# Two attentions on one core: value groups 4 to 7 of the dense units in one 512-column visit, the next x between the last Q and K

## The chip, the cores and the metric

One core of a Trainium2 chip. The metric is the device time of one execution in microseconds (us), median of several runs; lower is better. The engines are named as the profile names them: PE is TensorE (PEld its weight loads), DVE VectorE, ACT ScalarE, POOL GpSimd, SP SyncE.

## The reference

Two independent attentions over 2048 positions, model width 1024, 32 heads of 32. Each projects x to Q, K and V, attends and multiplies with wo; the two outputs stand side by side.

```
qkv = x @ wqkv                                   # (2048, 3072), q, k, v of 32 heads of 32
A: logits at keys pos - 0, 2, .., 14             # 8 keys, every second position
   softmax, weighted sum of v, @ wo
B: scores = q @ k.T / sqrt(32), masked to 0 <= i - j < 256
   softmax, @ v, @ wo
return concatenate([a, b], axis=-1)              # (1, 2048, 2048), float32
```

## The kernel before

The work is cut into eight units of 512 positions. Units 0 to 3 are B, the dense units; units 4 to 7 are A, the window units, whose positions are sorted into even and odd ones, so that the window of every second key becomes one of neighbours. A unit has eight groups of four heads (NG = 8); a group takes part as one "head" s below, and hg = 8 u + s numbers them through.

Every matmul of projections is made of three (TERMS): both operands are split into a high part, rounded to fp32r, and a rest, and high x high, high x rest and rest x high are added up. The split is made on the chip: a load of 512 KB lands in a tile of the ring `raws` (three tiles, tag raw), a cast on ACT (L213) or DVE (L216) makes the high part and two subtractions on DVE (L219) the rest, into the pools `wpool` (three tiles) or `xpool` (nine tiles of 512 columns, eight of which are one unit's x).

The projections form one list of visits, in the order of `plan`: per head a Q and a K visit (`qk_items`, L577, 8 steps of 3 matmuls of 512 columns each), value visits in between (`v_items`, L645), and for dense units the output projection of the unit before (`o_items`, L705). A value visit covers several groups at once. VPARTS says which: groups 0 to 3 in one wide visit (four weights of two k-steps by 512 columns; each of two rounds goes through the weights, and the first quarter is loaded and split twice, so five loads; matmuls of 512 columns), groups 4 and 5, and 6 and 7, in a narrow one each (two loads, matmuls of 256 columns). V_SLOTS says after which head's Q and K a visit stands: 0, 5 and 7 (V0_SLOTS for unit 0: 1, 3 and 7). The last narrow visit carries the arrival of the next unit's x: the four x loads are split after steps 1, 5, 9 and 13 (XAT = 1, m = 4), because the old x tiles come free one after the other.

Attention of a dense head runs in two halves: 16 score matmuls (L1078) for row maxima and sums (L1083 on DVE, L1088 on ACT), one small matmul for the row sums (L1117), which DVE spreads (L1123) into extra rows of Q, then transposed scores (L1161), exponentials (L1168), masks on POOL (L1147) or DVE (L1150), and the product with the values (L1208). A window head copies its rows from a tile of the ring `natp` (three tiles, tag nat) to its seat by SP's queue (pbuf<-nat), has many small score matmuls (L914), a chain on DVE and ACT (L922 to L964) in a buffer `band`, and the product with the values (L975).

The output projection of the window units is done at the end, for pairs of units (4 and 5, 6 and 7), as seven products (`product`, L764, 48 matmuls of 512 columns each) of sums of attention outputs with sums of weights. The sums are made in the background: `weight_sums` and `output_sums` load two pieces each by SP's queue (L832, r<-od, r<-wo), add on DVE (L837) and store again (L843) to sd and td, from where products load them like any other weight or x. Unit pair 4 and 5 had its `output_sums` after heads 4 to 7 of unit 5, pair 6 and 7 after heads 4 to 7 of unit 7.

The order of instructions on every engine is fixed when the program is made: a planner (class `Clock`) keeps an estimated time for each engine and each transfer, and always takes the one of four lists (row sums, second halves, first halves, projections) whose next item can start first. Loads go out on POOL's queue (`Stream.load_to`), each after the split that frees its tile; `split_to` makes the splits when a visit nears. A dictionary of gates holds loads back until their source is written. PE has three accumulator banks for projections (tag g), four for scores (s) and one for values (o).

## Time and profile before

| | |
|---|---|
| median of 3 runs | 1830.73 us (1830.16 to 1833.35) |
| the profiled execution's own time | 1835.97 us |
| its span | 1834.0 us |
| granted TensorE clock, mean | 0.991 |
| PE busy | 1799.3 us (98%) |
| DVE, ACT, POOL busy | 1262.2, 925.6, 409.2 us |
| DMA | 303.61 MB, mean 166 GB/s |

Busy time of an engine is the time in which at least one of its instructions runs. A row of a timeline gives the start, the duration, engine, line, operation, tiles and count, and in brackets the idle time before it with what ended it; runs of one operation are merged. A row of windows gives the busy time and instruction count of PE, PEld, DVE, ACT and POOL in a stretch, then the granted clock (PEclk, 1.00 is full), the DMA share and GB/s. A row of lines gives the busy time, the mean of one instruction in ns and the idle time ahead of it. "issue" means that the engine waited for nothing that the profile shows.

### The profile page before, as it was taken

The page shows a single profiled execution, that of the slowest core. Times are in us where ns is not written, and L with a number is a line of the kernel's source. Part 1 is how long each engine was busy: PE and PEld are TensorE (multiplying, and loading weights), DVE is VectorE, ACT ScalarE, POOL GpSimd, SP SyncE. Part 2 cuts the span into 40 slices and gives each one's busy share as a digit, 9 for nine tenths or more (in the row PEclk, how much of TensorE's full clock was granted, in tenths as well). Part 3 has the DMA queues.
Part 4 walks back from the last instruction along what each step waited for, and adds up shares of the span by engine and source line. Part 5 has one row for each costly group of instructions (what it writes and reads, how often), then busy time and mean ns, then how long its engine had stood idle before and what let it go on. Part 6 is the DMA issues. An engine that isn't in the chain of part 4 may idle for free. (4 is left out here: it accounts for less than half of the span.)

```text
span 1834.0 us, 38630 instructions
## 1 busy us (share of the span) xinstructions
PE 1799.3 (98%) x14730; PEld 1467.6 (80%) x14730; DVE 1262.2 (69%) x2789; ACT 925.6 (50%) x2302; POOL 409.2 (22%) x950
## 2 busy tenths in 40 slices
PE   9999999999999999999999999999989999999999
PEld 7787777888778888777887788888868888787777
DVE  6777876778867669777777565655765665657666
ACT  4556466565656655656555344533533543435343
POOL 2312323223242323332233200110010011001111
PEclk9999999999999999999999999999989999999999
DMA  8455655645655556455554344547775455347886
GB/s 240 114 146 135 180 164 143 176 121 153 170 151 163 140 151 182 125 155 144 141 141 130 110 148 131 156 144 251 239 230 165 127 159 159 123 153 252 263 251 197
DMA packets 129241, 303.61 MB, mean 166 GB/s; under 512 B 16160, under 2 KB 31520, under 8 KB 129056
## 3 DMA queue, kind: packets, MB, share of 16 engines
q0 software_dynamic: 45216, 164.65, 30.6%
q1 hardware_dynamic: 73472, 116.56, 22.6%
q10 hardware_dynamic: 10368, 19.93, 3.0%
q8 instruction: 117, 1.92, 0.5%
q14 instruction: 68, 0.56, 0.1%
HBM read 189.79 MB, written 44.04 MB: 127 GB/s over the span
## 5 line engine op out<-in xcount | busy, mean ns | idle before, releaser
L577 PE MATMUL g<-x,w 128*128 128x512 f32 x3072 | 774.2, 396 | 6.2 <-ACT x L213 2.0
L577 PEld LDWEIGHTS g<-x,w 128*128 128x128 f32 x3072 | 567.2, 189 | 118.7 <-issue 6.8
L219 DVE TENSOR_TENSOR w<-raw,w 128x512 fp32r<-128x512 f32 x518 | 339.9, 698 | 87.7 <-ACT w L213 80.9
L645 PE MATMUL g<-w,x 128*128 128x256 f32 (+1 forms) x2304 | 396.6, 323 | 0.5 <-issue 0.3
L645 PEld LDWEIGHTS g<-w,x 128*128 128x128 f32 x2304 | 337.0, 192 | 29.6 <-issue 1.4
L1088 ACT ACTIVATE s<-s,nm 128x384 f32<-128x384 f32 (+2 forms) x512 | 274.4, 537 | 102.5 <-DVE nm L1083 102.3
L1083 DVE CUSTOM_DVE_ANT_0 s<-s,mask_d 128x384 f32<-128x384 f32 (+2 forms) x512 | 261.8, 554 | 88.2 <-PE s L1078 87.6
L1147 POOL TENSOR_SCALAR_AFFINE_SELECT pbuf<-pbuf 128x128 f32<-128x128 f32 (+1 forms) x606 | 219.3, 390 | 327.1 <-ACT pbuf L1168 325.8
L1168 ACT ACTIVATE pbuf<-s 128x384 f32<-128x384 f32 (+2 forms) x480 | 202.8, 505 | 73.9 <-PE s L1161 71.7
L705 PE MATMUL g<-r,w 128*128 128x512 f32 x768 | 190.8, 394 | 1.4 <-ACT r L1043 0.7
L169 POOL DMA_DIRECT2D raw<-wqk x126 | 68.2, 541 | 442.0 <-DVE w L219 296.9
L764 PE MATMUL g<-x,w 128*128 128x512 f32 x672 | 159.2, 397 | 7.5 <-ACT w L213 6.4
L705 PEld LDWEIGHTS g<-r,w 128*128 128x128 f32 x768 | 141.9, 188 | 30.8 <-DVE r L1047 1.6
L764 PEld LDWEIGHTS g<-x,w 128*128 128x128 f32 x672 | 127.2, 191 | 39.0 <-ACT w L213 8.1
L1161 PEld LDWEIGHTS s<-qst,kst 128*128 128x128 f32 x704 | 113.2, 189 | 40.9 <-ACT s L1088 16.2
L1078 PE MATMUL s<-kst,qst 96*128 96x384 f32 (+2 forms) x512 | 142.5, 342 | 1.0 <-ACT s L1088 0.7
L216 DVE CAST w<-raw 128x1024 fp32r<-128x1024 f32 x186 | 128.4, 691 | 21.6 <-PE g L577 17.6
L1161 PE MATMUL s<-qst,kst 128*128 128x256 f32 (+2 forms) x704 | 136.5, 302 | 3.5 <-ACT s L1088 3.0
L1078 PEld LDWEIGHTS s<-kst,qst 96*128 96x128 f32 x512 | 93.4, 188 | 26.1 <-issue 4.3
L922 DVE TENSOR_TENSOR band<-s,near 128x160 f32<-128x160 f32 x128 | 32.5, 317 | 111.1 <-PE s L914 111.1
L213 ACT CAST w<-raw 128x1024 fp32r<-128x1024 f32 (+1 forms) x74 | 76.4, 1037 | 61.6 <-DMA raw<-wo 22.8
L1088 ACT ACTIVATION_READ_ACCUMULATOR s<-s,nm 128x1 f32 x512 | 105.3, 206 | 0.0
(80 smaller groups left out, 1409.2 us busy)
## 6 DMA issues: line engine op xcount, KB each, us to landing
raw<-wqk POOLq DMA_DIRECT2D x126, 512.0 KB, 4.4
raw<-wv POOLq DMA_DIRECT2D x72, 512.0 KB, 4.9
qst<-nat SPq DMA_DIRECT2D x96, 256.0 KB, 4.8
kst<-nat SPq DMA_DIRECT2D x96, 256.0 KB, 5.7
raw<-wo POOLq DMA_DIRECT2D x44, 512.0 KB, 4.4
raw<-xs POOLq DMA_DIRECT2D x28, 512.0 KB, 4.7
outs<-ost ACTq DMA_DIRECT2D x37, 256.0 KB, 3.0
kst<-halo SPq DMA_DIRECT2D x72, 128.0 KB, 4.5
```

Source lines behind the costliest of these rows:

```text
L216: nc.vector.tensor_copy(t[:, 0, :], raw)
L219: nc.vector.tensor_tensor(t[:, 1, c:c + 512], raw[:, c:c + 512], t[:, 0, c:c + 512].bitcast(F32), op=ALU.subtract)
L577: nc.tensor.matmul(h["ps"], h["w"][:, a, k * P:(k + 1) * P], xt[u][k][:, b, :], start=(k == 0 and i == 0), stop=(k == NK - 1 and i == 2))
L645: nc.tensor.matmul(ps, xt[u][kw * g + k][:, a, p0:p0 + P], h["w"][g][:, c, k], start=(first and t == 0 and half == 0), stop=(last and t == 2),
L705: nc.tensor.matmul(h["ps"], w[:, a, c:c + P], ot[u, k][:, b, :], start=(k == 0 and i == 0), stop=(k == NK - 1 and i == 2))
L764: nc.tensor.matmul(h["ps"], w[:, a, c:c + P], x[:, b, :], start=(k == 0 and t == 0), stop=(k == 3 and t == 2))
L1078: nc.tensor.matmul(ps[:, :n], q[0:96, j, b * P:(b + 1) * P], kk[0:96, j, c0:c1], start=True, stop=True)
L1083: nc.vector.tensor_tensor_reduce(ps[:, :n], ps[:, :n], mask[:, cut:full], scale=-1.0, scalar=BIG, op0=ALU.add, op1=ALU.min, accum_out=nm)
L1088: nc.scalar.activation(ps[:, :n], ps[:, :n], AF.Exp, bias=nm, scale=-1.0, accum_out=sm)
L1147: nc.gpsimd.affine_select(w, w, pattern=[[0, m], [step, n]], compare_op=ALU.is_ge, fill=0.0, base=base, channel_multiplier=chan)
L1161: nc.tensor.matmul(ps[:, i * n:(i + 1) * n], kk[:, j, 256 + kb * P:256 + (kb + 1) * P], q[:, j, q0:q0 + n], start=True, stop=True)
L1168: nc.scalar.activation(w, ps[:, :pack * n].rearrange("p (j n) -> p j n", j=pack), AF.Exp)
```

## The change

For dense units the value groups 4 to 7 become one wide visit, after head 5 (in unit 0 after head 4); window units keep their narrow visits. With no value visit after the last head, a dense unit's last Q and K are zipped step by step, and the next x is split between their steps (after steps 1, 5, 9 and 13 of the 16). The value buffer becomes two tiles of 512 columns. From the weights of the first product on, every other three loads use the three tiles of `natp`, gated on the last heads' copies, and splits ask for loads three places further ahead. `output_sums` of the first pair runs after heads 1 to 4 of unit 6. Product outputs that used tiles of the room pool go through `band`. In the instruction order of the changed program the value line has 768 matmuls of 256 columns less and 384 of 512 more, DVE eight more weight subtractions, and the outputs' additions 11 tiles moved from r to band.

```diff
-VPARTS = ((0,4),(4,2),(6,2))
-V_SLOTS = {0:0,5:1,7:2}
+VPARTS = {True: ((0, 4), (4, 4)), False: ((0, 4), (4, 2), (6, 2))}
+V_SLOTS = {True: {0: 0, 5: 1}, False: {0: 0, 5: 1, 7: 2}}
-V0_SLOTS = {1:0,3:1,7:2}
+V0_SLOTS = {1: 0, 4: 1}
...
+        self.wide = len(items)
...
-            raw = self.more[k] if 0 <= k < len(self.more) else self.raws.tile([P, 1024], F32, tag="raw", name="raw")
+            if self.loaded >= self.wide and (self.loaded - self.wide) % (2 * NRAW) < NRAW:
+                raw = self.room()
+            else:
+                raw = self.more[k] if 0 <= k < len(self.more) else self.raws.tile([P, 1024], F32, tag="raw", name="raw")
...
-            self.ck.defer(end, lambda n=i + m + NRAW + 1 if i < NRAW else max(2 * NRAW + m, i + NRAW + 1): self.load_to(n))
+            deep = NRAW if i >= self.wide - NRAW else 0
+            self.ck.defer(end, lambda n=i + m + NRAW + 1 if i < NRAW else max(2 * NRAW + m, i + NRAW + deep + 1): self.load_to(n))
...
+    last_dense = DU * NG - 1
+    st.wide = where["p", DU, 0, "t", 0]
+    st.room = lambda: natp.tile([P, 2 * S + 16], F32R, tag="nat", name="raw").bitcast(F32)[:, :2 * S]
+    for i in range(NN):
+        gates[st.wide + i] = landed("nat", U * NG + last_dense + 1 - NN + i)
...
-    vbuf = [const.tile([P, 6, n * P], F32, name=f"vbuf{i}") for i, (_, n) in enumerate(VPARTS)]
+    vbuf = [const.tile([P, 6, 4 * P], F32, name=f"vbuf{i}") for i in range(2)]
...
-                o = slot(2 + where_o["ot"] % 2)[:, :S] if where_o["ot"] % 3 else stp.tile([P, S], F32, tag="ost", name="ost")
+                o = band[where_o["ot"] % 2][:, 1024:1536] if where_o["ot"] % 3 else stp.tile([P, S], F32, tag="ost", name="ost")
...
-                    if s >= 4 and u % 2:
+                    if u == U - 1 and s >= 4:
                         output_sums(u - 1, s - 4)
+                    if u == U - 2 and 0 < s < 5:
+                        output_sums(DU, s - 1)
...
-            if NG - 1 not in V_SLOTS and p[2] == NG - 1 and p[1] + 1 < U:
+            if NG - 1 not in V_SLOTS[units[p[1]][2]] and p[2] == NG - 1 and p[1] + 1 < U:
+                new = [i for pair in zip(new[:NK], new[NK:]) for i in pair]
                 for g, x in reversed(list(enumerate(x_items(p[1] + 1)))):
-                    new[NK + 2 * g:NK + 2 * g] = x
+                    new[4 * g + XAT:4 * g + XAT] = x
...
-            if V_SLOTS.get(NG - 1) == p[2] and p[1] + 1 < U:
-                m = 2 * VPARTS[p[2]][1]
+            if V_SLOTS[units[p[1]][2]].get(NG - 1) == p[2] and p[1] + 1 < U:
+                m = 4
```

The other lines of the diff look up VPARTS, V_SLOTS and the value tile by the kind of the unit.

More of the change, by code (lines that the diff above doesn't have):

```diff
@@ L265 @@
             plan.append(("qk", u, s))
-            vs = V_SLOTS if u else V0_SLOTS
+            vs = V_SLOTS[units[u][2]] if u else V0_SLOTS
             if s in vs:
@@ L325 @@
         elif p[0] == "v":
-            s0, n = VPARTS[p[2]]
+            s0, n = VPARTS[units[p[1]][2]][p[2]]
             for i, g in enumerate((0, 1) if n == 2 else (0, 1, 2, 3, 0)):
@@ L337 @@
         else:
-            if NG - 1 in V_SLOTS:
+            if NG - 1 in V_SLOTS[units[p[1] - 1][2]]:
                 item(("qk", p[1], 0, 0), "w", wqk[units[p[1]][0], 0])
@@ L409 @@
     pfree = [0.0]
-    vbuf = [const.tile([P, 6, n * P], F32, name=f"vbuf{i}") for i, (_, n) in enumerate(VPARTS)]
-    vpart = {s0 + i: (p, i * P) for p, (s0, n) in enumerate(VPARTS) for i in range(n)}
+    vbuf = [const.tile([P, 6, 4 * P], F32, name=f"vbuf{i}") for i in range(2)]
+    vpart = {(d, s0 + i): p for d in VPARTS for p, (s0, n) in enumerate(VPARTS[d]) for i in range(n)}
     tails = const.tile([P, NG, 8], F32, name="tails")
@@ L414 @@
     band, wide = [None, None], [None, None]
-    last_dense = sum(NG for u in units if u[2]) - 1
     halo = [[dram.tile([P, 2, 256], F32, name=f"halo{i}_{s}") for s in range(NG)] for i in range(2)]
@@ L611, in v_items @@
         h = {"w": {}}
-        s0, ng = VPARTS[part]
+        s0, ng = VPARTS[units[u][2]][part]
         wide = ng == 4
@@ L667, in after @@
                 c = (4 * u + (2 * r + b if wide else 2 * b)) % 6
-                t = copy_out(vbuf[part][:, c:c + per, :], h[b][0].rearrange("p (a f) -> p a f", a=per), h[b][1], rg)
+                to = s0 % 4 * P
+                t = copy_out(vbuf[s0 // 4][:, c:c + per, to:to + ng * P], h[b][0].rearrange("p (a f) -> p a f", a=per), h[b][1], rg)
                 done["vt", r, b] = t
@@ L889, in window @@
         hg = u * NG + s
-        vp, vc = vpart[s]
-        v = vbuf[vp]
+        vp, vc = vpart[units[u][2], s], s % 4 * P
+        v = vbuf[s // 4]
         def p64():
@@ L1061, in attention @@
         q, kk = qst[buf], kst[buf]
-        vp, vc = vpart[s]
-        v = vbuf[vp]
+        vp, vc = vpart[units[u][2], s], s % 4 * P
+        v = vbuf[s // 4]
         h = {"left": 16, "rows": None}
```

## The prediction

> **What bounds the kernel now.** First the page: which engine has no room.
>
> ```profile
> span 1834.0 us, 38630 instructions
> ...
> PE 1799.3 (98%) x14730; PEld 1467.6 (80%) x14730; DVE 1262.2 (69%) x2789; ACT 925.6 (50%) x2302; POOL 409.2 (22%) x950
> ...
> q8 instruction: 117, 1.92, 0.5%
> ```
>
> TensorE (PE) is busy in 98% of the span, so time comes only from fewer or shorter matmuls, from PE's waits, and from stretches at a lower clock. All waits together are 1834.0 - 1799.3 = 34.7 us. So next I read the timeline of PE for the waits of some length (start, duration, operation; in brackets the wait before it and what ended it):
>
> ```profile
> 171.53 0.45 PE L1078 MATMUL s<-kst,qst 96*128 96x384 f32 x1 [0.74 <-ACT s L1088]
> 174.58 0.44 PE L1161 MATMUL s<-qst,kst 128*128 128x128 f32 x2 [0.33 <-ACT pbuf L1168]
> 180.29 0.22 PE L1117 MATMUL s<-ident,hl 128*32 128x128 f32 x1 [1.99 <-DVE hl L1109]
> 204.12 1.80 PE L1161 MATMUL s<-qst,kst 128*128 128x256 f32 x8 [1.14 <-ACT s L1088]
> 712.68 0.82 PE L1161 MATMUL s<-qst,kst 128*128 128x128 f32 x4 [0.61 <-ACT s L1088]
> 721.54 0.22 PE L1117 MATMUL s<-ident,hl 128*32 128x128 f32 x1 [0.59 <-DVE hl L1109]
> 1342.23 1.43 PE L577 MATMUL g<-x,w 128*128 128x512 f32 x5 [0.84 <-DVE x L219]
> 1345.28 0.73 PE L577 MATMUL g<-x,w 128*128 128x512 f32 x2 [1.62 <-ACT w L213]
> 1347.48 3.04 PE L577 MATMUL g<-x,w 128*128 128x512 f32 x7 [1.47 <-DVE w L219]
> 1368.81 0.35 PE L914 MATMUL s<-pbuf 32*32 32x40 f32 x6 [2.44 <-issue]
> 1605.97 0.65 PE L975 MATMUL o<-wide,vbuf 128*32 128x136 f32 x13 [2.58 <-issue]
> 1677.23 3.23 PE L764 MATMUL g<-x,w 128*128 128x512 f32 x9 [2.95 <-ACT w L213]
> 1706.27 13.90 PE L764 MATMUL g<-x,w 128*128 128x512 f32 x53 [3.50 <-ACT w L213]
> 1747.02 11.25 PE L764 MATMUL g<-x,w 128*128 128x512 f32 x48 [0.79 <-DVE r L782]
> ```
>
> These are five places: the end of unit 0 (171 to 204), the change of x between dense units (712 to 722, and a like place in each unit), the change from unit 5 to 6 (1342 to 1348), two waits for nothing visible ("issue"), and the products at the end (1677 to 1747). Then the windows, for the clock behind the waits (after the busy times stand PEclk, the DMA share and GB/s):
>
> ```profile
> 180.30:184.00 3.70, 3.70 (x19) 3.70 (x20) 3.38 (x6) 1.09 (x2) 0.00 (x0) 0.54 1.03 231
> 420.00:480.00 60.00, 59.04 (x390) 48.89 (x382) 53.60 (x129) 33.29 (x95) 20.34 (x41) 1.00 0.64 175
> 1342.00:1351.50 9.50, 6.18 (x42) 4.01 (x46) 8.09 (x16) 6.86 (x12) 1.43 (x2) 0.82 0.81 268
> 1368.40:1375.20 6.80, 6.39 (x20) 4.97 (x20) 5.34 (x10) 1.17 (x2) 0.00 (x0) 0.50 0.39 142
> 1679.00:1682.40 3.40, 3.40 (x10) 2.66 (x9) 3.30 (x6) 1.54 (x4) 0.55 (x1) 0.50 0.49 154
> 1706.30:1709.70 3.40, 3.40 (x8) 2.68 (x9) 3.29 (x6) 1.56 (x2) 0.53 (x1) 0.50 0.48 152
> 1655.00:1760.00 105.00, 97.54 (x620) 78.41 (x619) 73.31 (x121) 45.72 (x72) 18.62 (x32) 0.97 0.80 255
> ```
>
> Behind a wait of 2 us or more, or several close together, the granted clock is 0.50 for 3.4 us (6.8 us behind the one at 1368.81). That is 3.4 x 0.5 = 1.7 us of lost work, added to the wait. The waits of 0.6 us at 712 and 721 I charge alone.
>
> **The change part by part.**
>
> *One value visit of 512 columns for groups 4 to 7.* In each of the four dense units it removes 192 matmuls of 256 columns and adds 96 of 512: 768 less, 384 more. What each form occupies is read from start to start on the timeline:
>
> ```profile
> 37.56 2.24 PE L645 MATMUL g<-w,x 128*128 128x512 f32 x9
> 39.64 0.63 PE L1078 MATMUL s<-kst,qst 96*128 96x384 f32 x2
> ...
> 99.99 2.31 PE L645 MATMUL g<-w,x 128*128 128x256 f32 x18
> 102.14 0.34 PE L1078 MATMUL s<-kst,qst 96*128 96x384 f32 x1
> ```
>
> Nine wide ones take 39.64 - 37.56 = 2.08 us, the 18 narrow ones with the same work 102.14 - 99.99 = 2.15 us. 384 / 9 x 0.07 = 3.0 us are saved, all on the path, since PE is the bound. The Trainium skill ("TensorE: Matmul & The Clock Gate", Back-to-back issue gap) gives N / 2.4 + 2.5 ns between matmuls when warm. By that, only 2.5 ns would go with each of 384 matmuls, 1.0 us in place of 3.0; I keep the rows.
>
> The wide visit loads the first quarter of its weights twice: five loads and splits for four. These are its costs (mean ns of one stands behind the busy time):
>
> ```profile
> L219 DVE TENSOR_TENSOR w<-raw,w 128x512 fp32r<-128x512 f32 x518 | 339.9, 698 | 87.7 <-ACT w L213 80.9
> L216 DVE CAST w<-raw 128x1024 fp32r<-128x1024 f32 x186 | 128.4, 691 | 21.6 <-PE g L577 17.6
> L219 DVE TENSOR_TENSOR x<-raw,x 128x512 fp32r<-128x512 f32 x116 | 76.3, 691 | 31.8 <-ACT x L213 30.6
> L216 DVE CAST x<-raw 128x512 fp32r<-128x512 f32 x35 | 18.4, 526 | 3.5 <-DMA raw<-xs 2.8 <-PE o L1208 0.7
> ```
>
> One split is 0.69 + 2 x 0.70 = 2.1 us of VectorE (DVE) per unit. It lies beside a visit of 96 x 0.231 = 22 us of matmuls, and is free unless DVE is the pace there (third rival). The evictions stay four of 512 columns. The added load stands on POOL's queue among the mask operations (L1147) of the dense heads, one issue more per unit: 0.
>
> *Next x between the last Q and K.* The x splits lay among the value visit of groups 6 and 7, four steps of the visit apart; now they lie four steps apart in the last Q and K visit. Either visit is 48 matmul times of 512 columns, 11 us, and the amount of DVE work is the same. So the three later changes of x keep their loss of about 1.2 us each (0.61 + 0.59): 0. Bounds: all of it gone, -3.6; or each as bad as the end of unit 0 now, 3 x (5.9 - 1.2) = +14.
>
> *End of unit 0.* It loses 0.74 + 0.33 + 1.99 + 1.14 = 4.2 us and 1.7 of clock, 5.9. The order of the changed kernel's instructions still has a poor stretch there: between the 6th and the 7th row-sum matmul (L1117) stand 30 projection matmuls, as between the 5th and 6th now, followed by eight score matmuls (L1161) in a row that go at the pace of their evictions. I take 0, between -5.9 (the stretch goes) and +5.9 (it comes twice).
>
> *Sums of the first unit pair.* They ran after heads 4 to 7 of unit 5 and now run after heads 1 to 4 of unit 6. The four additions of one stand exactly ahead of the split that PE waits for at 1342:
>
> ```profile
> 1338.71 2.87 DVE L837 TENSOR_TENSOR r<-r 128x512 f32<-128x512 f32 x4
> 1341.49 1.28 DVE L219 TENSOR_TENSOR x<-raw,x 128x512 fp32r<-128x512 f32 x2
> ```
>
> With DMA at 0.81 in that window, the loads of x and the next weights were late too. All three waits go, 0.84 + 1.62 + 1.47 = 3.9, and the clock's 1.7: -5.6. In the new place there is no x to load. What they meet there is the seat copies on SP's queue (pbuf<-nat), behind which window scores wait; PE has projections for that time. Bounds: -5.6, or the same loss in the new place, 0.
>
> *Six loads ahead in the products.* The products begin and end so:
>
> ```profile
> 1662.61 11.68 PE L764 MATMUL g<-x,w 128*128 128x512 f32 x48
> ...
> 1758.49 71.82 PE L764 MATMUL g<-x,w 128*128 128x512 f32 x312 [0.23 <-DVE r L782]
> ```
>
> From 1662.6 to 1830.3 they wait 2.95 + 3.50 + 0.79 + 0.23 = 7.5 us, with the half clock twice (3.4): 10.9 us. The cause is the ring of three raw tiles, in the timeline and in the list of waits from 1655 to 1760 (us in total, times, longest):
>
> ```profile
> 1660.43 0.73 POOL L169 DMA_DIRECT2D raw<-wo  x1 [7.27 <-DVE x L219]
> ...
> 1667.17 1.05 ACT L213 CAST w<-raw 128x1024 fp32r<-128x1024 f32 x1 [3.80 <-DMA raw<-wo]
> ...
> ACT w L213 <- DMA raw<-wo: 16.4, 6, 3.8
> ```
>
> The POOL queue waits for a split to free a tile, then the load needs over 6 us, and the cast waits for it. A product of 48 matmuls (11.1 us) needs four such loads. With three tiles more (the three nat tiles, free once the last heads' rows are copied) loads start up to three places earlier, 3/4 of 11.1 = 8 us, more than the longest wait of 3.5. The first of them wait, on POOL's queue, for the seat copies of heads 61 to 63; behind them there queue only further loads, and who waits for those is the second product, a visit later. The DMA share of 0.80 over 105 us is 84 us of work, which still fits into 95. I take -8.0, leaving about 3 us for the last sums, which still run then. Bounds: -10.9 and 0. The output tiles moved to band have to wait for head 63's spread (L961); two other accumulator banks, 2 x 2.8 us, cover that.
>
> *"Issue" waits.* 1.92 MB in 117 code loads for 2 x 14730 matmuls and weight loads are about 252 instructions each. I read the two waits as PE running out of code where many short matmuls stand together. The change takes out 2 x 384 = 768 instructions ahead of them, three loads of 256, so later code lies about as before within its loads: 0. Bounds: both gone, 2.44 + 3.4 + 2.58 + 1.7 = -10.1; one more, +4.3.
>
> Sum: -3.0 - 5.6 - 8.0 = -16.6 us. The profiled execution's own time is 1835.97 us (span 1834.0), which would become 1819.4. The median of the runs, 1830.73, lies 5.2 lower; with the same savings it becomes 1814.1. The Trainium skill (same page, HAM oscillation) ties the fall to half clock to idle gaps above about 3.4 us. The rows differ: 1.99 and 2.95 us were enough. By that rule only the 3.50 us wait would cost clock, and the sum would be 3.4 less, -13.2.
>
> **The rivals.**
>
> *The products keep waiting.* If w and x tiles or the sums' transfers (r<-od) set the pace and not the raw ring, the 8.0 stays: -8.6, 1822. Against it: in the list of waits it is a landing DMA that the casts wait for. Chance 0.18.
>
> *The sums stall unit 6.* They move through DMA and DVE between the loads of weights; if PE loses there what it lost at 1342: -11.0, 1820. Against it: the new place has a free clock, hardly a wait and half the DMA now:
>
> ```profile
> 1380.00:1440.00 60.00, 59.92 (x710) 48.87 (x709) 36.84 (x66) 24.59 (x47) 5.29 (x10) 1.00 0.48 148
> ```
>
> Chance 0.12.
>
> *DVE becomes the pace at the changes of x (slower).* DVE is at 53.60 of 60 in the window at 420, where x changes. One change is 8 x (0.53 + 0.69) = 9.7 us of splits; with the added weight split and side by side Q and K, which ask for two accumulators at once, these could lie open. If each of four places lost the whole 9.7 in place of 5.9 + 3 x 1.2 = 9.5 together, that is +29.3, net +12.7: 1843. It decides from 16.6 + 9.5 = 26.1, 6.5 us a place. For it: the stretch of 30 matmuls. Against it: the amount of work per visit hardly differs. Chance 0.10.
>
> **How the numbers follow.** The forecast, 1814, has 0.60. About 0.2% (3.7 us) is what a measurement here tells from no change. The range reaches up to 1828, over the first two rivals, with the third and some mixtures outside; down to 1805, for the end of unit 0 or part of the issue waits gone. Faster needs below 1827.1: forecast and the first two rivals give 0.90, of which 0.05 falls back by a loss at the changes of x. Faster 0.85, same 0.05, slower 0.10.
>
> **What would show it.** Right: no wait above 1 us on L764, no half clock between 1640 and the end; none on L577 at the change from unit 5 to 6; 768 matmuls of 256 columns less on the value line, and its 512 form still 0.231 us (2.08 / 9) from start to start; DVE's window at the changes of x below 55 of 60. Wrong: waits <-DVE x L219 above 3 us at a change of x, a new run of waits in unit 6, or products still behind raw loads.

## The result, and the profile after

The changed kernel takes 1846.33 us (median of 4 runs, 1843.36 to 1851.15); the kernel before took 1832.04 us in the same rounds. The ratio is 1.0081, 95% interval 1.0056 to 1.0106: by that ratio it is slower by 14.8 us, where 16.6 us less had been forecast. The profiled execution took 1851.15 us, with a span of 1849.4.

From the page after: the span, the busy times, and the groups of the value matmuls (L654) and of the products (L774; the last number is the idle time ahead of them).

```profile
span 1849.4 us, 37850 instructions
...
PE 1807.4 (98%) x14346; PEld 1452.6 (79%) x14346; DVE 1266.8 (68%) x2779; ACT 922.0 (50%) x2293; POOL 428.2 (23%) x985
...
L654 PE MATMUL g<-w,x 128*128 128x512 f32 (+1 forms) x1920 | 394.0, 352 | 5.1 <-DVE w L224 4.6
...
L774 PE MATMUL g<-x,w 128*128 128x512 f32 x672 | 154.3, 392 | 0.0
```

384 matmuls are gone and the products wait for nothing, as forecast. Yet PE is busy for 8.1 us longer (1799.3 before) and waits 42.0 us in place of 34.7. Four windows show where it is not lost: the end of the run (from the first product on), and the change from unit 5 to 6. The first two rows are of the kernel before, the next two of the changed one.

```profile
1662.60:1830.30 167.70, 160.21 (x716) 128.16 (x712) 113.25 (x184) 65.14 (x95) 29.60 (x52) 0.98 0.77 243
1335.30:1385.70 50.40, 44.03 (x483) 33.98 (x482) 35.31 (x58) 22.24 (x42) 5.96 (x10) 0.90 0.63 203
```

```profile
1690.30:1845.80 155.50, 155.46 (x716) 127.78 (x712) 114.38 (x188) 63.52 (x93) 28.52 (x50) 0.99 0.76 262
1372.50:1410.80 38.30, 37.25 (x355) 30.05 (x354) 25.63 (x44) 19.85 (x38) 5.49 (x9) 1.00 0.44 141
```

These two gave back 12.2 and 12.1 us. (In the second, 128 of the small score matmuls had been done earlier in the changed kernel, 483 against 355 matmuls; at 43.3 us for 4096 of them in the kernel before, that is about 1.4 us of the 12.1.) So the changed kernel entered them late: its first product starts at 1690.3, not at 1662.6, and unit 6 at 1372.5, not at 1335.3. Most of this lag is built up in the dense units: it is 35.4 us at head 3 of unit 4, the first window unit. The window from 8 to 1010 us, before and after:

```profile
8.00:1010.00 1002.00, 992.02 (x5986) 801.98 (x5987) 748.95 (x1927) 582.70 (x1678) 300.20 (x742) 0.99 0.56 152
```

```profile
8.00:1010.00 1002.00, 973.58 (x5403) 762.19 (x5404) 729.57 (x1858) 563.31 (x1621) 302.35 (x753) 0.98 0.54 152
```

PE waited 10.0 us of these 1002 before (1002.00 - 992.02) and 28.4 us after, and the granted clock fell from 0.99 to 0.98. VectorE (DVE) was *less* busy in the same stretch: 729.57 us against 748.95. The list of PE's waits after, from 120 to 1020 us (us in total, times, longest), shows no single culprit:

```profile
PE s L1090 <- ACT s L1100: 5.7, 6, 1.2
PE g L654 <- DVE w L224: 4.6, 6, 1.1
PE s L1090 <- DMA kst<-halo: 4.0, 2, 2.1
PE s L1173 <- DVE qst L1135: 3.6, 5, 1.5
PE s L1129 <- DVE hl L1121: 1.9, 1, 1.9
PE s L1090 <- DMA halo<-nat: 1.9, 1, 1.9
PE s L1090 <- issue: 1.8, 3, 1.4
```

One change of x, from PE's timeline (unit 2 to 3), and what the clock did behind two of its waits:

```profile
675.20 1.92 PE L654 MATMUL g<-w,x 128*128 128x512 f32 x5 [0.82 <-DVE w L224]
723.96 0.94 PE L1090 MATMUL s<-kst,qst 96*128 96x384 f32 x4 [1.90 <-DMA halo<-nat]
739.24 1.57 PE L1090 MATMUL s<-kst,qst 96*128 96x384 f32 x3 [1.25 <-ACT s L1100]
753.98 2.12 PE L654 MATMUL g<-w,x 128*128 128x512 f32 x8 [1.13 <-DVE w L224]
```

```profile
675.90:679.40 3.50, 3.50 (x13) 2.92 (x12) 0.29 (x2) 1.58 (x6) 0.10 (x1) 0.51 0.42 154
740.80:744.20 3.40, 3.40 (x10) 2.69 (x9) 3.00 (x11) 2.75 (x10) 0.05 (x1) 0.50 0.96 308
700.00:760.00 60.00, 55.48 (x301) 43.25 (x300) 48.44 (x110) 28.15 (x79) 20.56 (x42) 0.97 0.60 171
```

Waits of 0.8 and 1.3 us are followed by a half clock of 3.4 us, which costs 1.7 more. DVE is at 48 of 60 us in the window from 700 to 760, less than the 53.60 before, in the window at 420.

The start of the Q matmuls of head 3 in each unit gives the lag behind the kernel before: 13.5 us in unit 1, 17.5 in unit 2, 26.8 in unit 3, 35.4 in unit 4. The first of these is not all loss. At that point the changed kernel has done 64 attention matmuls more (166, 176 and 352 on L1090, L1173 and L1220, where the kernel before has 162, 164 and 304); at the three later points it is ahead by two at most. Up to there it has waited 2.6 us longer and lost 3.4 us more to the half clock; the other 7 us or so of the 13.5 are, by estimate, this work done sooner. So unit 0 with its change of x costs about 6 us, unit 1 with its own about 11, and units 2 and 3 with theirs 9.3 and 8.6.

### The profile page after: what moved, and what is told of

Same layout as the page of the kernel before. It is cut to its first block, busy times and chain, and to the rows that moved or that the text cites. A ratio compares the mean times of both kernels' runs of the same rounds, so it can differ in the third digit from the quotient of the medians.

```text
span 1849.4 us, 37850 instructions
## 1 busy us (share of the span) xinstructions
PE 1807.4 (98%) x14346; PEld 1452.6 (79%) x14346; DVE 1266.8 (68%) x2779; ACT 922.0 (50%) x2293; POOL 428.2 (23%) x985
## 5 line engine op out<-in xcount | busy, mean ns | idle before, releaser
L586 PE MATMUL g<-x,w 128*128 128x512 f32 x3072 | 777.4, 399 | 2.9 <-ACT x L218 2.0
L586 PEld LDWEIGHTS g<-x,w 128*128 128x128 f32 x3072 | 574.9, 191 | 117.8 <-issue 6.9
L654 PE MATMUL g<-w,x 128*128 128x512 f32 (+1 forms) x1920 | 394.0, 352 | 5.1 <-DVE w L224 4.6
L224 DVE TENSOR_TENSOR w<-raw,w 128x512 fp32r<-128x512 f32 x526 | 344.6, 697 | 48.1 <-ACT w L218 41.3
L654 PEld LDWEIGHTS g<-w,x 128*128 128x128 f32 x1920 | 305.6, 190 | 47.2 <-DVE w L224 8.1
L1159 POOL TENSOR_SCALAR_AFFINE_SELECT pbuf<-pbuf 128x128 f32<-128x128 f32 (+1 forms) x637 | 230.1, 390 | 279.3 <-ACT pbuf L1180 277.2
L221 DVE CAST w<-raw 128x1024 fp32r<-128x1024 f32 x192 | 133.3, 694 | 43.4 <-PE g L586 28.3
L1090 PE MATMUL s<-kst,qst 96*128 96x384 f32 (+2 forms) x512 | 148.0, 346 | 14.4 <-ACT s L1100 5.7
L774 PE MATMUL g<-x,w 128*128 128x512 f32 x672 | 154.3, 392 | 0.0
L1173 PEld LDWEIGHTS s<-qst,kst 128*128 128x128 f32 x704 | 115.1, 192 | 48.0 <-ACT s L1100 13.2
L774 PEld LDWEIGHTS g<-x,w 128*128 128x128 f32 x672 | 126.8, 189 | 27.2 <-issue 0.6
L1173 PE MATMUL s<-qst,kst 128*128 128x256 f32 (+2 forms) x704 | 139.8, 309 | 5.3 <-DVE qst L1135 3.6
L1090 PEld LDWEIGHTS s<-kst,qst 96*128 96x128 f32 x512 | 94.9, 190 | 44.8 <-ACT s L1100 15.2
L173 POOL DMA_DIRECT2D raw<-wv x76 | 52.0, 684 | 297.0 <-DVE w L224 169.0
```

Source lines behind the costliest of these rows:

```text
L221: nc.vector.tensor_copy(t[:, 0, :], raw)
L224: nc.vector.tensor_tensor(t[:, 1, c:c + 512], raw[:, c:c + 512], t[:, 0, c:c + 512].bitcast(F32), op=ALU.subtract)
L586: nc.tensor.matmul(h["ps"], h["w"][:, a, k * P:(k + 1) * P], xt[u][k][:, b, :], start=(k == 0 and i == 0), stop=(k == NK - 1 and i == 2))
L654: nc.tensor.matmul(ps, xt[u][kw * g + k][:, a, p0:p0 + P], h["w"][g][:, c, k], start=(first and t == 0 and half == 0), stop=(last and t == 2),
L774: nc.tensor.matmul(h["ps"], w[:, a, c:c + P], x[:, b, :], start=(k == 0 and t == 0), stop=(k == 3 and t == 2))
L1090: nc.tensor.matmul(ps[:, :n], q[0:96, j, b * P:(b + 1) * P], kk[0:96, j, c0:c1], start=True, stop=True)
```

## The experiments

Edits are against the changed kernel if nothing else is said. Differences between two kernels of different rounds are taken between their ratios to the kernel before, times 1830.7 us, with the intervals added in squares.

**First, the parts alone, the last head's order, and narrow visits.** (The letters of the theories in these first four texts are not those used later.)

The changes at the end of the run alone (raw tiles, moved sums, output tiles):

```diff
-VPARTS = {True: ((0, 4), (4, 4)), ...
-V_SLOTS = {True: {0: 0, 5: 1}, ...
-V0_SLOTS = {1: 0, 4: 1}
+VPARTS = {True: ((0, 4), (4, 2), (6, 2)), ...
+V_SLOTS = {True: {0: 0, 5: 1, 7: 2}, ...
+V0_SLOTS = {1: 0, 3: 1, 7: 2}
```

> The dense units as before (three value visits, x under the last one); kept of the change: six raw tiles in the products, sums of the first pair after heads 1 to 4 of unit 6, outputs in band. Theory (the end gains, the dense units lose): the changed kernel caught up 36 us of its lag after unit 5 began to 15 at the end, so this one is some 21 us faster than before, about 1810. Rival (the later parts gained only because the dense units shifted them, or the gain was scatter of code loading): 1820 to 1832.

Measured: 1816.14 us, ratio 0.9914 [0.9885, 0.9944]: 15.7 us faster than the kernel before, and the lowest of all versions.

The dense part alone:

```diff
-            if self.loaded >= self.wide and (...) % (2 * NRAW) < NRAW:
+            if False:
...
-            deep = NRAW if i >= self.wide - NRAW else 0
+            deep = 0
... (the gates of the nat tiles go, and outputs use the room pool again)
-                    if u == U - 1 and s >= 4:
+                    if s >= 4 and u % 2:
                         output_sums(u - 1, s - 4)
-                    if u == U - 2 and 0 < s < 5:
-                        output_sums(DU, s - 1)
```

> The reverse: wide dense visits and x between the last Q and K as in the changed kernel; raw ring, sums and outputs as before. Theory: the dense units alone lose some 35 us, so about 1866. Rival (the deeper loads or the moved sums make the dense units' plan worse): less than 1850.

Measured: 1860.83 us, 1.0163 [1.0115, 1.0211]. The parts add up: -0.0086 + 0.0163 = 0.0077, against 0.0081 for both. The dense part costs about 30 us.

The last Q ahead of the last K, x within K:

```diff
-                new = [i for pair in zip(new[:NK], new[NK:]) for i in pair]
...
-                    new[4 * g + XAT:4 * g + XAT] = x
+                    new[NK + 2 * g:NK + 2 * g] = x
```

> The changed kernel with the last Q of a dense unit in front of its K, the next x between the steps of K alone. Theory A (the side by side order is the loss: it bunches copies and evictions): the dense units lose little, about 1812. Theory B (the 22 us visit in one piece is the loss: it keeps attention without new heads and bunches them at the change of x): still 1840 or more.

Measured: 1849.94 us, 1.0095 [1.0065, 1.0125], no difference in the end. The lag is spread a little differently: 2.6 us behind unit 0, with as many attention matmuls done as in the kernel before (changed kernel: about 6), then 14.5, 22.5 and 30.4: 12, 8 and 8 in units 1 to 3.

Narrow visits after heads 5 and 6, x as in the changed kernel:

```diff
-VPARTS = {True: ((0, 4), (4, 4)), ...
-V_SLOTS = {True: {0: 0, 5: 1}, ...
-V0_SLOTS = {1: 0, 4: 1}
+VPARTS = {True: ((0, 4), (4, 2), (6, 2)), ...
+V_SLOTS = {True: {0: 0, 5: 1, 6: 2}, ...
+V0_SLOTS = {1: 0, 3: 1, 6: 2}
```

> The changed kernel with two narrow visits in dense units again, after heads 5 and 6 (unit 0: 3 and 6); x between the last Q and K side by side. Theory A (side by side with x is the loss): still 1840 or more. Theory B (the wide visit in one piece): about 1812, the end's gain with a small loss.

Measured: 1831.73 us, 0.9993 [0.9972, 1.0013]. Taking x out of the last value visit (which then comes a head sooner) costs 14.5 +- 6.5 us against the version with the end alone; the rest of the 30 belongs to the value visits.

**Where the visit stands, and DVE.** Letters from here on: A, the spread of the projections over the heads; B, the visit itself; C, DVE's pace.

```diff
-V_SLOTS = {True: {0: 0, 5: 1}, ...
+V_SLOTS = {True: {0: 0, 6: 1}, ...
```

> The changed kernel with one edit: in units 1 to 3 the wide value visit of groups 4 to 7 comes after head 6, not after head 5 (unit 0 as it was). So far the dense part of the change costs about 30 us (1846.3 against 1816.1 with only the changes at the end), some 14 of them in unit 0. Theory A: the loss in the later units is a matter of where the projections lie. In the changed order 75, 138 and 84 projection matmuls stand between the row-sum matmuls 14 to 17; with this edit the most is 129, and around it stand 84 and 87, with 102, 96 and 96 ahead. By A each of units 1 to 3 loses about 3 us less: about 1838, and fewer waits for scores, spread rows and halo at the change of x. Theory B: the wide visit costs where it stands, because it holds three weight tiles and the next weights come late (waits of the value matmuls on VectorE's w): 1846, the loss per unit as in the changed kernel. Theory C: VectorE is the pace: 1846 too, since its work is the same.

```diff
-V_SLOTS = {True: {0: 0, 5: 1}, ...
+V_SLOTS = {True: {0: 0, 4: 1}, ...
```

> The changed kernel with one edit: in units 1 to 3 the wide value visit comes after head 4, a head earlier. In this order 81, 228 and 9 projection matmuls stand between row-sum matmuls 13 to 16 (changed kernel: about 100, 75, 138). Theory A (the loss comes from projections piled in one place, so that two heads' attention stands nearly bare in the next): clearly slower than the changed kernel, by 5 us or more per unit, 1860 or more, with waits for scores and spread rows where the 9 stand. Theory B (the form and its three held weight tiles cost, wherever it stands) and theory C (VectorE's amount of work is the pace): 1846, within 4.

Measured: after head 6 1847.47 us, 1.0072 [1.0052, 1.0093], no gain, though the projections lie more evenly; after head 4 1867.51 us, 1.0190 [1.0170, 1.0209], 20 us worse. The weights' waits are gone after head 6, and others stand in their place; the first row of this kernel's list of waits, of the row sums for hl:

```profile
PE s L1129 <- DVE hl L1121: 7.5, 3, 2.8
```

A bad pile (228 projections, then 9) costs a lot, as theory A said for this run. But with the more even order after head 6 nothing is gained, so unevenness doesn't explain the loss of the changed kernel.

The casts given to ScalarE where that ends no later:

```diff
-SIDE_X, SIDE_W = -99, -99
+SIDE_X, SIDE_W = 0.0, 0.0
```

> The changed kernel with one edit: the planner gives the cast of a raw tile to ScalarE wherever that would end no later than on VectorE (until now nearly all casts of the dense stages stay on VectorE). This takes some 0.5 to 0.7 us of VectorE work off many splits, and evens the order as well (the row-sum matmuls 14 to 17 have 78, 117 and 99 projections between them, not 75, 138 and 84). Theory C (VectorE is the pace at the changes of x, the third rival of the prediction): most of the dense loss of 30 us goes, 1825 or less, and the waits of the value matmuls on VectorE's w with it. Theory A (spread of the projections): a part of it, 1838 to 1842. Theory B (the held weight tiles): 1846 or more, since ScalarE's casts take 1.05 us in place of 0.69 and its row work has to wait for them.

Measured: 1839.27 us, 1.0031 [1.0020, 1.0042]: 9 +- 5 us better than the changed kernel. That lies in A's range (by the ratio, at 1836.4, just under it) and far from the 1825 or less of C. The same edit on the version with the end alone:

> The version with only the changes at the end of the run (1816.1 where the kernel before took 1830.3), with the casts of raw tiles given to ScalarE where that ends no later, as in the run before, where it took 7 us off the changed kernel. Theory C (VectorE's queue is what the dense stages wait behind): another 3 us or more, 1813 or less. Theory A2 (the spread of projections over the heads decides; here 96 and 135 at the changes of x in place of 108 and 96): no gain or a loss, 1816 to 1822.

Measured: 1828.02 us, 0.9983 [0.9968, 0.9998]: 12.6 +- 6 us *worse* than without it. DVE has 36 us less to do in the one (1266.8 to 1231.0 us busy) and 40 us less in the other (1261.6 to 1222.0), ScalarE some 50 more in each. Less work on DVE alone does not bring the time back, so C falls as the one explanation.

The loads alone, without the moved sums (dense stages as before):

```diff
 (on the version with the end alone)
-                    if u == U - 1 and s >= 4:
+                    if s >= 4 and u % 2:
                         output_sums(u - 1, s - 4)
-                    if u == U - 2 and 0 < s < 5:
-                        output_sums(DU, s - 1)
```

> Of the change only the six raw tiles of the products and the output tiles in band; dense stages and the place of the unit pair's sums as in the kernel before. The version with the moved sums as well took 1816.1 where the kernel before took 1830.3, -14.2. The prediction gave -8.0 to the loads and -5.6 to the moved sums. If so, this one takes 1822, with the three waits at the change from unit 5 to 6 as before. If the sums' place carries more (about 11 us came back at the change from unit 5 to 6), 1826; if the loads carry nearly all, 1817.

Measured: 1824.26 us, 0.9950 [0.9931, 0.9969]. The loads bring 9.2 +- 3.5 us, the sums the other 6.6 +- 6.4. Its timeline has the waits at the change of unit that the sums make, nearly as before:

```profile
1342.74 1.44 PE L586 MATMUL g<-x,w 128*128 128x512 f32 x5 [0.67 <-DVE x L224]
1345.80 0.74 PE L586 MATMUL g<-x,w 128*128 128x512 f32 x2 [1.62 <-ACT w L218]
1348.00 3.12 PE L586 MATMUL g<-x,w 128*128 128x512 f32 x7 [1.46 <-DVE w L224]
```

**A chain that reads well, and is not the cause.** In the changed kernel's trace one can follow the 1.90 us at 723.96 back. DVE's timeline, then SP's queue:

```profile
711.46 0.69 DVE L224 TENSOR_TENSOR x<-raw,x 128x512 fp32r<-128x512 f32 x1
716.32 0.48 DVE L221 CAST x<-raw 128x512 fp32r<-128x512 f32 x1 [4.17 <-PE g L586]
716.83 0.69 DVE L224 TENSOR_TENSOR x<-raw,x 128x512 fp32r<-128x512 f32 x1
717.44 0.69 DVE L527 SCALAR_TENSOR_TENSOR nat<-g,nat 128x512 fp32r<-128x512 f32 x1
```

```profile
712.46 6.24 SPq L547 DMA_DIRECT2D kst<-nat  x3
718.75 0.74 SPq L537 DMA_DIRECT2D halo<-nat  x1
```

The cast of a new x tile stands in DVE's queue for 4.17 us, because PE still reads the old tile in its place. Behind it stands the low half of the keys (L527), behind that their copies on SP's queue, and the scores wait for one of these. So the split of x was put behind the matmuls that free the tiles:

```diff
-                    new[4 * g + XAT:4 * g + XAT] = x
+                    new[4 * g + 4:4 * g + 4] = x
```

> The changed kernel with one edit: between the last Q and K of a dense unit, the split of a pair of new x tiles comes behind the matmuls that free both tiles, three steps later. In the trace of the changed kernel VectorE stands up to 4.2 us in front of the cast of x, because the next of the nine x tiles is still read by TensorE (13.0 us in four waits over units 1 to 3; nearly nothing in the kernel before), and behind it stand the low half of K and so the stacked keys that the next scores wait for. Theory D (this wait in VectorE's order is the loss at the change of x): the waits of the casts go, the scores no longer wait for kst, 2 us and the half clock of 1.7 at each change: about 1836. Theory A2 (too few projections for the heads behind the wide visit): the wait turns up elsewhere, 1844 to 1849.

Measured: 1853.78 us, 1.0117 [1.0085, 1.0150]. Between 180 and 1010 us the casts' waits on PE go from 13.0 to 4.4 us, and the time does not come back. The waits of the dense stages are on other rows (this kernel, 120 to 1020 us):

```profile
PE s L1090 <- ACT s L1100: 5.3, 6, 1.2
PE s L1129 <- DVE hl L1121: 4.7, 2, 3.5
PE s L1173 <- DVE qst L1135: 4.0, 3, 1.6
```

Theory D of the text above falls: the wait was there, but when it was taken away others of the same size stood in its place.

**What part of the wide visit costs.** Two narrow visits, one behind the other, in the wide one's place:

```diff
-VPARTS = {True: ((0, 4), (4, 4)), ...
-V_SLOTS = {True: {0: 0, 5: 1}, ...      V0_SLOTS = {1: 0, 4: 1}
+VPARTS = {True: ((0, 4), (4, 2), (6, 2)), ...
+V_SLOTS = {True: {0: (0,), 5: (1, 2)}, ...      V0_SLOTS = {1: (0,), 4: (1, 2)}
...
-                plan.append(("v", u, vs[s]))
+            for part in vs.get(s, ()):
+                plan.append(("v", u, part))
...
```

> The changed kernel with the values of groups 4 to 7 as two visits of 256 columns, both in the place of the wide one (after head 5, in unit 0 after head 4), one right behind the other; x stays between the last Q and K. So the projections lie as in the changed kernel (96, 84, 123, 84 between row-sum matmuls, changed kernel 90, 75, 138, 84), but heads 4 and 5 get their values half a visit earlier, each weight is loaded once, and no weight tile is held through a second round. Theory B2 (the one wide visit is itself at fault: it holds back the attention of heads 4 and 5 until its end and keeps three weight tiles): each of units 1 to 3 loses 2 us as with visits after heads 5 and 6, and the total is 1832 to 1836, though the 256-column form costs some 4 us more. Theory A2 (22 us of projections in one place leave too few for the heads behind it, whichever form): 1846 to 1851.

Measured: 1838.59 us, 1.0045 [1.0023, 1.0066], between the two theories: 9.5 +- 5.5 us more than with visits after heads 5 and 6, and 6.6 +- 6 less than the changed kernel. Then the same, with heads 4 and 5 released only at the end of the second visit:

```diff
+    ends = {}
...
-                    done["v"][u, part] = max(...)
+                    ends[u, part] = max(...)
+                    if not units[u][2] or part != 1:
+                        for i in ((part,) if part != 2 or not units[u][2] else (1, 2)):
+                            done["v"][u, i] = max(ends[u, i], ends[u, part])
```

> The kernel with two visits of 256 columns one behind the other in the place of the wide one (1838.6), with one edit: in the dense units the values of heads 4 and 5 are given free to the planner only when the second of the two visits ends, as the one wide visit does it. The matmuls, loads, splits and evictions are the same; no weight tile is held longer. In its order 72 to 81, 153 and 69 projections stand between row-sum matmuls 14 to 17 (without the edit 84 to 93, 123 and 84, changed kernel 75, 138, 84). Theory B2a (the wide visit costs because it holds back the attention of heads 4 and 5 until its end): 8 us or more slower, 1846 to 1855, with some 8 us or more lost in each of units 1 to 3 as in the changed kernel (without the edit 3 to 4). Theory B2b (it costs by the weight tiles that it holds and the fifth load): as without the edit, 1838, within 4.

Measured: 1835.74 us, 1.0020 [1.0007, 1.0032]: no loss. The late release falls, and with it what was left of A: in this order 153 projections stand in one place, where the changed kernel has 138 at most. Then two narrow visits with the fifth load and split added, unread:

```diff
+                    if units[p[1]][2] and p[2] == 2 and i == 1:
+                        item(p + (2,), "w", wv[ly, 4])
...
+            if ("v", u, part, 2) in where and not wide and n == 1 and k == 3 and b == 0:
+                st.get(where["v", u, part, 2])
+                ahead(where["v", u, part, 2] + 1)
```

> The kernel with two narrow visits one behind the other after head 5 (1838.6), with one thing added: behind the second visit of each dense unit one more weight (the first quarter's) is loaded and split into a w tile that nobody reads. This is the fifth load and split of the wide visit by itself: 0.69 + 2 x 0.65 us of VectorE and one issue on the POOL queue a unit. The prediction took it as free. Theory B2b (the wide visit's extra load counts): 2 us or more a unit, 1846 or more. Theory E: within 4 of 1838.6.

Measured: 1847.60 us, 1.0083 [1.0057, 1.0109]: 7.0 +- 6.2 us, just clear of zero, for four loads and splits that nobody reads; this is as slow as the changed kernel. And the wide visit with its weights asked for sooner:

```diff
-                if k == 0 and b == 1 and n < 3:
-                    ahead(item_of(n + 1))
+                if n == 0 and k == 0 and b == 0:
+                    ahead(item_of(1))
+                if n < 2 and done_block:
+                    ahead(item_of(n + 2))
```

> The changed kernel with one edit: in the first round of a wide value visit each next quarter of the weights is asked for as soon as its tile is free, some 1 to 3 us sooner than now (it applies to the visits of groups 0 to 3 and of groups 4 to 7). In the changed kernel the value matmuls wait 4.6 us for VectorE's w in units 1 to 3 (six waits, the longest 1.1), with the half clock behind one of them. Theory B2b (the wide visit loses against two narrow ones in its place because its weights come late): these waits go, and with them 6 to 8 us: 1838 to 1841. Theory E (no single wait is the cause: whichever is taken away, the moved order of VectorE's and ScalarE's work makes another of the same size): 1843 to 1850, with new waits on other rows.

Measured: 1836.05 us, 1.0020 [1.0001, 1.0039]: 11 +- 6 us off the changed kernel. Two rows of its waits (120 to 1020 us), and the dense window:

```profile
PE s L1092 <- ACT s L1102: 5.1, 6, 1.2
...
PE g L654 <- DVE w L224: 0.9, 1, 0.9
```

```profile
8.00:1010.00 1002.00, 983.26 (x5502) 770.96 (x5503) 742.26 (x1895) 572.86 (x1651) 312.34 (x756) 0.99 0.55 153
```

The waits for w fall from 4.6 to 0.9 us, but all waits of the window from 28.4 to 18.7. That the late weights made the others late, and the clock low, fits this; the run doesn't show it by itself. Which visits carry this:

```diff
 (in the visits of groups 4 to 7 alone: the new lines under "part == 1", the old one under "part != 1")
```

> The changed kernel with the weights asked for sooner in the wide visit of groups 4 to 7 alone; the visits of groups 0 to 3 ask as before. With both it took 1836.1, without 1846.3. Theory B2b: the visit of groups 4 to 7 carries it, 1835 to 1839. If the visits of groups 0 to 3 carry it: 1844 to 1847.

```diff
 (on the version with the end alone, so in the visits of groups 0 to 3)
```

> The best version so far (dense stages as in the kernel before, the changes at the end of the run kept: 1816.1), with the weights of the wide value visits of groups 0 to 3 asked for sooner, as in the run before, where it took 10 us off the changed kernel. In this version no value matmul of units 1 to 3 waits for more than 0.2 us. Theory B2b (the gain there came from the waits of the visit of groups 4 to 7): no gain, 1814 to 1819. Theory E (each change of the order makes other waits): 1820 or more. If the visits of groups 0 to 3 were late as well: 1806 to 1812.

Measured: 1841.52 us, 1.0060 [1.0037, 1.0083], 3.8 +- 6.2 us off the changed kernel, not clear of none, and 7.3 +- 5.5 us short of what both visits together gave; and 1819.03 us, 0.9927 [0.9898, 0.9955], no gain. The visits of groups 0 to 3 bring nothing by themselves, and the new visit alone doesn't bring the whole. How the two add up stays open.

Last, narrow visits after heads 5 and 6 with the last Q ahead of K:

```diff
 (on the version with narrow visits after heads 5 and 6)
-                new = [i for pair in zip(new[:NK], new[NK:]) for i in pair]
...
-                    new[4 * g + XAT:4 * g + XAT] = x
+                    new[NK + 2 * g:NK + 2 * g] = x
```

> The kernel with narrow visits after heads 5 and 6 and the next x between the last Q and K side by side (1831.7; with the dense part as in the kernel before 1816.1), with one edit: the last Q comes ahead of the last K, and x stands among K alone. It tells apart the two things that this kernel still changes in the dense part. If Q and K side by side cost the 15.6 us (they stretch the last head's Q, and both accumulators stay taken): 1816 to 1821. If the cost is that x lies between Q and K and no longer in a value visit, or that groups 6 and 7 are visited a head sooner: 1828 to 1834.

Measured: 1841.49 us, 1.0042 [1.0026, 1.0057], 9 +- 5 us worse than side by side, outside both expectations. With narrow visits, Q and K side by side are the better form, so nothing here shows that this form costs. What remains for the 14.5 us is x's new place and the sooner visit of groups 6 and 7. These two were not taken apart.

## Why the prediction was wrong

Against the version with only the end of the run changed, the changed kernel's dense part costs 30.6 +- 7 us; forecast was -3.0. Two profiles say in what coin. Here are the span and the mean granted clock of the changed kernel, then of that version with its busy times and its dense window:

```profile
core 0: 1849.4 us, clock 0.988
```

```profile
core 0: 1813.4 us, clock 0.998
```

```profile
PE 1786.9 (99%) x14730; PEld 1461.4 (81%) x14730; DVE 1261.6 (70%) x2790; ACT 924.4 (51%) x2301; POOL 410.5 (23%) x950
```

```profile
8.00:1010.00 1002.00, 991.07 (x5992) 800.37 (x5992) 749.87 (x1930) 583.82 (x1682) 301.46 (x743) 1.00 0.56 152
```

Waits: 42.0 - 26.5 = 15.5 us more (1813.4 - 1786.9 = 26.5). Clock: (1 - 0.988) x 1849.4 = 22.2 us lost against 0.002 x 1813.4 = 3.6, so 18.6 more. The difference of the spans is 36.0. In these two profiles about half of the loss sat inside "busy 98%", as matmuls at half clock. But they are the longest of the four executions of the changed kernel and the shortest of the five of the other. The mean granted clock of all the executions is 0.9915 and 0.996, which is 15.7 us lost against 7.3: about 8 of the 30.6 us.

- *Wide form, -3.0*: right in itself. Nine wide matmuls go from 691.97 to 694.02, 0.228 us each (0.231 forecast), as these rows of the timeline after show:

```profile
691.97 2.22 PE L654 MATMUL g<-w,x 128*128 128x512 f32 x9
694.02 0.84 PE L586 MATMUL g<-x,w 128*128 128x512 f32 x3
```

- *"These are its costs... free unless DVE is the pace"*: the step that failed first. The fifth load and split cost about 7 us in the order in which they were tried alone, where their DVE time is 4 x 2.1 = 8.4 us: as if almost none were hidden, though DVE has about 20% free even in the window from 700 to 760. The price was worked out by amounts. That the wait is one of order, at the moment when the next weight is due, fits the 11 us that asking sooner brought back; it isn't shown beyond that.
- *"Next x between the last Q and K: 0... the amount of DVE work is the same"*: the step that failed worst, with the sooner visit of groups 6 and 7 that it silently took along: +14.5. The stated bounds for this and the end of unit 0 (-9.5 to +20) held it, the value chosen did not. That both visits stand in one place costs another 9.5, which had no term at all; even with both bounds at their worst the sum would have been 1834.
- *End of unit 0, 0 within +-5.9*: about +6 us with its change of x, at the bound. The 30 bare projections that the prediction pointed at came with six waits of 0.4 us and more, 6.6 us together (four of them in the rows below), and with the half clock for twice its length behind one of them (the window below), a loss of another 3.4. That is 10.0 us, where the kernel before lost 5.9:

```profile
134.15 0.41 PE L1173 MATMUL s<-qst,kst 128*128 128x384 f32 x1 [1.54 <-DVE qst L1135]
184.68 0.45 PE L1090 MATMUL s<-kst,qst 96*128 96x384 f32 x1 [0.78 <-ACT s L1100]
200.68 0.41 PE L1173 MATMUL s<-qst,kst 128*128 128x384 f32 x1 [1.45 <-DVE qst L1135]
216.83 0.22 PE L1129 MATMUL s<-ident,hl 128*32 128x128 f32 x1 [1.93 <-DVE hl L1121]
```

```profile
201.50:208.30 6.80, 6.68 (x17) 5.28 (x18) 5.78 (x17) 5.39 (x17) 5.09 (x13) 0.50 0.25 80
```

- *Sums moved, -5.6*: right in mechanism. The three waits on L577 (now L586) and the half clock are gone, and between the version with the loads alone and the one with the sums too lie 6.6 +- 6.4 us.
- *Six loads ahead, -8.0*: right, 9.2 +- 3.5 measured; the products wait for nothing. The half clock that was to be gone after 1640 came once, from 1689.69 to 1693.10, behind a wait of 1.9 us ahead of the first product.
- *"Issue" waits, 0*: both are gone in the changed kernel, the one at 1368.81 with its half clock, which is why the change from unit 5 to 6 gave some 11 us and not 5.6. That one is still there with the loads alone (1.89 us at 1368.8) and gone with the sums moved too, both with the dense stages as before: so it went with the sums, not with the 768 instructions. The one at 1605.97 stays in both (2.44 and 2.73 us). Why they come and go isn't shown.
- *The rivals*: the third named the side, the place and nearly the time (1843), at a chance of 0.10. That was luck: its mechanism, DVE's amount, isn't borne out, since taking casts off DVE helped one order by 9 us and hurt another by 12.6. The two milder rivals did not occur.

The fault of method was to carry the loss of one order (1.2 us at each change of x) over to another because the work was the same. The waits of a static order are a property of the order. What the runs support, not as one cause but as a sum: x's place and the sooner visit 14.5, both visits together 9.5, the fifth load 7, the wide form about none beyond these, all with errors of about 6 us. These are steps from one order to the next; in another order the same edit can be worth something else, as the casts were. What in the orders makes the waits stays open. Of the three experiments that took one kind of wait away from the changed kernel, by the place of the visit, of x, or of the request for weights, two gained nothing and one 11 us.

## What to carry to other kernels

In a kernel that keeps its busiest engine at 98% with an order fixed in advance, price a reordering by the bounds, not by "same work, same cost": fifteen orders of the same dense stages, all with the end as changed, lay between 1816 and 1868 us here. Add to each expected wait what the clock can lose behind it, and read busy time together with the granted clock. Take a change apart before judging it: the edits at the end of the run were worth 15.7 us, and the dense ones cost twice that.

## What the runs showed of the hardware

The clock falls to half behind shorter waits than forecast, and not behind each. A wait of 0.82 us (with three of 0.2 to 0.5 in the 6 us ahead of it) and one of 1.25 us were enough, at 675.20 and 739.24; behind 1.90 us at 723.96 and 1.54 us at 134.15 it stayed full. The longest wait of the dense units, 2.09 us at 456.61, was followed by the half clock too. So the length of the last wait alone does not decide.

The clock records show what does for the most part. In all nineteen profiles each change of the clock lies on an even grid with steps of 3.41 us (two half clocks of the changed kernel begin at 457.48 and 474.55, five steps apart), and what PE idles within one step of it counts together. Here are two steps ahead of a half clock, and the two steps on which the wait of 1.54 us lies:

```profile
672.53:675.94 3.41, 2.06 (x10) 1.43 (x9) 3.35 (x8) 1.56 (x5) 2.18 (x3) 1.00 0.01 2
737.38:740.79 3.41, 1.92 (x7) 0.98 (x6) 3.38 (x8) 2.77 (x9) 0.67 (x1) 1.00 1.08 220
129.81:133.22 3.41, 2.80 (x13) 1.89 (x11) 1.93 (x3) 0.00 (x0) 0.00 (x0) 1.00 1.04 250
133.22:136.63 3.41, 2.48 (x12) 2.25 (x13) 2.54 (x5) 1.22 (x3) 1.61 (x5) 1.00 0.61 175
```

Step less busy time, PE idles 1.35 and 1.49 us in the first two, and 0.61 and 0.93 in the others: the wait of 1.54 us lies across a border and counts in two parts. The limit isn't sharp: the step at 720.31, with most of the wait of 1.90 us, has 1.66 us idle and the full clock behind it. Of the steps at full clock in the nineteen profiles (without the first 25 and the last 8 us), all 40 with 2.0 us idle or more have the half clock behind them, 26 of 29 with 1.8 to 2.0, 36 of 103 with 1.2 to 1.8, and 10 of 9735 with less. So what a wait costs also hangs on where it meets the grid. The grid lies differently against the start in each profile: the first half clock begins at 9.86 us in the kernel before, at 10.34 in the changed one, and at 11.08 with only the end changed. That fits the clocks of 0.988 to 0.993 in four executions of the same changed kernel, though it isn't shown to be their cause.

The Trainium skill ("TensorE: Matmul & The Clock Gate", HAM oscillation) ties the fall to idle gaps above about 3.4 us. No wait of the changed kernel is that long, so the measurement goes against it here.
